# A block of products on constant tiles ahead of the first stage of a gated attention and feed-forward training step

## The chip, the core and the metric

One core of a Trainium2 chip runs the kernel. Five engines work side by side, each through its own list of instructions in order: TensorE (PE in the profile, its weight loads PEld), VectorE (DVE), ScalarE (ACT), GpSimd (POOL) and SyncE (SP). Transfers are issued from the queues of SP, ACT and POOL. Engines wait for each other through semaphores. The metric is the device time of one execution in microseconds, lower is better.

## What is computed

The reference is a mix of two branches on one input x (2048 rows, 512 columns, bf16), and the kernel returns the forward result and seven gradients:

```python
g = _sigmoid((x * gate_w).sum(-1, keepdims=True))
a = _A_ref(x, A_wqkv, A_wo)                  # attention, 32 heads of 16, window of 256, causal
b = _B_ref(x, B_W_gate, B_W_up, B_W_down)    # h = relu(x @ W_gate) * (x @ W_up), then h @ W_down, F = 1376
out = g * a + (1 - g) * b
...
_out, _vjp = jax.vjp(_f, A_x, A_wqkv, A_wo, B_W_gate, B_W_up, B_W_down, gate_w)
_grads = _vjp(grad_out)
```

The gradients are those of x, of the five weight matrices and of gate_w.

## The kernel before

The rows are cut into 16 tiles of 128, taken four at a time (tg, 512 rows: TGW), and the 1376 columns of the feed-forward branch into 11 pieces of 128 (fc). Three stages follow each other.

The first stage is the feed-forward branch forward and backward. 44 steps (11 pieces by 4 row groups) each make `gate` and `up` (products of Wg_sb and Wu_sb with x_T, L326), `dh` (product of WdT with db_T, L326 too), and six steps later the weight gradients (`weights`, L373 and L375). The results h and the two gradients are turned by transfers on SP's queue (`turn_h`, `turn_dgu`) and kept in memory by transfers on ACT's queue (`keep`). The second stage is attention: scores, exponentials, masks and their gradients, tile by tile, with the projections of later groups and the weight gradients laid between by a hand-written order with credits. The third stage takes two row tiles at a time and makes the output and the gradient of x.

Both the first and the second stage stand under an order written out by hand: instructions come on each engine in the order in which the code issues them.

Around the change the start of the first stage matters. In this order: VectorE fills the tile `warm` with zeros (L222); SP loads the first 512 rows of x in two halves (L225), while ACT's queue loads the first 256 columns of each weight (Wg_sb L226, Wu_sb L227) and gw_col (L228); ACT loads its table for the sigmoid (L230); POOL makes `ident`; PE does eight products of `warm` with itself, WARM = 8 (L234). Then SP loads the rest of x (L237) and the rows of grad_out (L213, into the tiles z), turns the first piece of W_down (L219) and loads the remaining columns of both weights (L247, L248). With the first rows there, `turn_x(0)` turns x on PE (tile ptx, L261), and VectorE and ACT each evict one half (L74, L72). Step 0 follows: `gate`, `turn_x(1)`, `up`, `gate_col` (L269, the tile zps, needs gw_col and gives g_all through a sigmoid), `db_rows` (L279 and L281, on ACT and VectorE), and a step later `turn_db` (tile ptd, L289). In the first four steps x and db are turned between the products; from then on a step is products alone.

The first-stage tiles db_r, db_T, Wg_sb, Wu_sb and gw_col come from the pool `acts` on the left side of the memory, which is opened with the stage; x_r, x_T and the z tiles lie elsewhere. The products' results lie in the pool ps1 of eight banks: three for products (tag mm), two for turns (tag tr), three for sums of weight gradients.

Of the kernel before, what the change touches and what calls it, by code (L numbers as in the profile page):

```python
# [11 lines left out]
BF = mybir.dt.bfloat16  # L12
F32 = mybir.dt.float32
I32 = mybir.dt.int32
PSUM = bass.MemoryType.PSUM
# [7 lines left out]
def kernel(  # L23
# [20 lines left out]
    nc = tc.nc  # L44
    P = 128
# [13 lines left out]
    TGW = min(512, S)  # L59
# [7 lines left out]
    def evac(out, in_, eng=None):  # L67
        if eng is None:
            eng = ("act", "dve")[rr["i"] % 2]
            rr["i"] += 1  # L70
        if eng == "act":
            nc.scalar.copy(out, in_)  # L72
        elif eng == "dve":
            nc.vector.tensor_copy(out, in_)  # L74
        else:
            nc.gpsimd.tensor_copy(out, in_)
# [36 lines left out]
    if True:  # L113
        HH = HG // 2
        proj = {}
        groups = [(c, tg) for c in range(DC) for tg in range(NTG)]
        PENG = ("dvs", "dvs")

        def project_parts(c, tg):
            t4 = {}  # L120
            proj[(c, tg)] = t4
            pj = pjA if (c * NTG + tg) % 3 == 0 else pjs["b"]

            def mm(nm, which, eng):
                ps, tag, bufs, _ = pools["now"]
                pp = ps.tile([P, TGW], F32, tag=tag, bufs=bufs, name="pp")
                for cd in range(DC):
                    if which < 3:
                        nc.tensor.matmul(pp[:], lhsT=w_p[c][:, cd, which * P:(which + 1) * P], rhs=x_T[tg][:, cd, :],  # L129
                                         start=(cd == 0), stop=(cd == DC - 1))  # L130
                    else:
                        nc.tensor.matmul(pp[:], lhsT=w_p[c][:, cd, 3 * P:4 * P], rhs=da_T[tg][:, cd, :],
                                         start=(cd == 0), stop=(cd == DC - 1))
                if nm in ("Q", "dO"):
                    if nm == "Q":
                        t4["z"] = pjA.tile([P, 2, TGW], BF, tag="zT", name="zT")
                    dst = t4["z"][:, ("Q", "dO").index(nm), :]
                else:
                    dst = pjA.tile([P, TGW], BF, tag="T", bufs=2, name=f"{nm}T")[:]
                if nm == "Q":  # L140
                    nc.vector.tensor_scalar(dst, pp[:], scale, None, op0=ALU.mult)
                else:
                    evac(dst, pp[:], eng)
                t4[nm] = dst
                if nm in ("Q", "dO"):
                    if c == 0 and tg == 0:
                        w = ("Q", "dO").index(nm)
                        for k in range(NP):
                            rows = slice(32 * k, 32 * k + 32)
                            evac(zt[0][rows, w, :, k, :], dst[rows, :].rearrange("p (k q) -> p k q", k=TPG),  # L150
                                 (("dve", "act")[w] if k % 2 else "dve"))
                else:
                    for k in range(2):
                        t4[f"{nm}{k}"] = pj.tile([P, TGW], BF, tag=f"{nm}{k}", name=f"{nm}{k}")
                        if PENG[k] == "act":
                            nc.scalar.mul(t4[f"{nm}{k}"][:], pp[:], par[:, k:k + 1])
                        elif PENG[k] == "dve":
                            nc.vector.tensor_scalar(t4[f"{nm}{k}"][:], pp[:], par[:, k:k + 1], None, op0=ALU.mult)
                        else:
                            nc.vector.tensor_scalar(t4[f"{nm}{k}"][:], dst[:], par[:, k:k + 1], None, op0=ALU.mult)  # L160

            def tr(a_nm, b_nm):
                ps, tag, bufs, trt = pools["now"]
                pt = ps.tile([P, 2, TPG, P], BF, tag=trt, bufs=2, name="ptp")
                for a, nm in enumerate((a_nm, b_nm)):
                    for k in range(TPG):
                        nc.tensor.transpose(pt[:, a, k, :], t4[nm][:, k * P:(k + 1) * P], ident[:])
                return pt

            def tr_rows():  # L170
                rows = pjA.tile([P, 2, TPG, P], BF, tag="rows", bufs=2, name="rows")
                nc.sync.dma_start_transpose(out=rows[:].rearrange("p a t d -> p (a t) d"),
                                            in_=t4["z"][:].rearrange("p a s -> p (a s)"))
                t4["rows"] = rows

            def tr_kv():
                kv = pj.tile([P, TPG, HG, 34], BF, tag="KV1", name="KV1")
                nc.gpsimd.memset(kv[:, :, :, 0:1], -1.0)
                nc.gpsimd.memset(kv[:, :, :, Dh + 1:Dh + 2], 1.0)
                pt = tr("K", "V")  # L180
                v = lambda a: pt[:, a, :, :].rearrange("p k (h d) -> p k h d", h=HG)
                nc.vector.tensor_scalar(kv[:, :, :, 1:1 + Dh], v(0), scale, None, op0=ALU.mult)
                nc.vector.tensor_copy(kv[:, :, :, Dh + 2:2 * Dh + 2], v(1))
                t4["kv"] = kv

            return [lambda: mm("Q", 0, "dve"), lambda: mm("dO", 3, "dve"), tr_rows, lambda: mm("K", 1, "act"),
                    lambda: mm("V", 2, "act"), tr_kv]

    with ExitStack() as p1, tc.manual_schedule():
        ps1 = p1.enter_context(tc.tile_pool(name="ps1", bufs=1, space=PSUM))  # L190
# [120 lines left out]
        for fc in range(FC):  # L311
            for tg in range(NTG):
                k = Step()
# [90 lines left out]
        for n in range(N1 + 8):  # L404
# [22 lines left out]
            if at(6):  # L427
                f = weights(at(6))
# [14 lines left out]
            if t in (NT + 3, NT + 5):  # L443
                i = (t - NT - 3) // 2
                nc.gpsimd.memset(zt[i][:, 0, :, :, :], 0.0)
                nc.vector.memset(zt[i][:, 1, :, :, :], 0.0)
            if n == N1 - 2:
                first = project_parts(*groups[0])
# [10 lines left out]
    if True:  # L459
# [340 lines left out]
        with tc.manual_schedule():  # L800
# [7 lines left out]
            n = 0  # L808
# [12 lines left out]
            while n <= NU + LAG or ev or cdq or bgq:  # L821
# [5 lines left out]
                if u is not None:  # L827
                    gi = u.c * NTG + u.j // TPG
                    if u.first and u.j == 0:
                        sts[u.c] = st.tile([P, NT, 4, P], BF, tag="rows_st", name="rows_st")  # L830
                    if u.first and u.j % TPG == 0:
                        if gi + 1 < len(groups):
                            prq = project_parts(*groups[gi + 1])
                            due = n + sum(2 * min(3, j + 1) for j in range(u.j, u.j + TPG)) - 3
                            if gi + 2 == len(groups):
                                due -= 10
                    if u.first and u.j == 6 and u.c > 0:
                        ev.setdefault(n + 1, []).append(("dma", lambda c=u.c - 1: spill(c, NT // 2)))
                    if u.first and u.j == 1 and u.c > 0:
                        ready = grad_parts(u.c - 1)  # L840
                    if u.first and u.j == TPG - 1 and u.c > 0:
                        bgq += ready
                    front(u)
                    if u.last and gi + 1 == len(groups) and u.j % TPG in (1, 3):
                        ev.setdefault(n + 2, []).append(("dma", lambda i=(u.j % TPG) // 2: early_f(i)))
# [7 lines left out]
                if LAG <= n < NU + LAG:  # L853
                    w = units[n - LAG]
# [65 lines left out]
    with ExitStack() as p56:  # L920
        x_r5 = x_r

        with ExitStack() as p6:
# [5 lines left out]
            for g in range(NG):  # L929
# [3 lines left out]
                for tl in range(GT):  # L933
# [4 lines left out]
                    for fc in range(FC):  # L938
                        nc.tensor.matmul(bps[:], lhsT=hT_g[:, fc, lsl], rhs=W6[("Wd", fc)],  # L939
                                         start=(fc == 0), stop=(fc == FC - 1))  # L940
                    aps = ps6.tile([P, D], F32, tag="aps", bufs=1)
                    for c in range(DC):
                        nc.tensor.matmul(aps[:], lhsT=T_g[:, 4 * c + 3, lsl], rhs=W6[("wo", c)],
                                         start=(c == 0), stop=(c == DC - 1))
# [20 lines left out]
                    i = 0  # L965
                    for src, wt in ((dgT_g, "Wg"), (duT_g, "Wu")):
                        for fc in range(FC):
                            nc.tensor.matmul(dxps[:], lhsT=src[:, fc, lsl], rhs=W6[(wt, fc)],  # L968
                                             start=(i == 0), stop=(i == nmm - 1))
# [14 lines left out]
                    for cc in range(C3):  # L984
                        nc.tensor.matmul(dxps[:], lhsT=T_g[:, 4 * (cc % DC) + cc // DC, lsl], rhs=W6[("wqkv", cc)],  # L985
                                         start=(i == 0), stop=(i == nmm - 1))
# [35 lines left out]
```

## Time and profile before

| | before |
|---|---|
| median of two runs | 978.9 us (978.26 to 979.54) |
| span of the profiled execution | 976.6 us |
| PE busy, products | 936.5 us, 11280 products |
| PE weight loads busy | 597.0 us |
| VectorE, ACT, POOL busy | 500.5, 473.1, 488.0 us |
| mean granted TensorE clock | 0.993 |
| moved by DMA | 161.6 MB, 166 GB/s on the mean |

A row of the profile's order of time has the start, the length, the engine, the line in the code, the operation, what it writes and reads by tile names, the array's part as rows*columns, the shape, the count of instructions taken together, and in brackets how long the engine was idle before it and what ended that. The length of a single product is counted to the end of its way through the array; products overlap, so the time between two starts, not the length, is what one product takes from the engine. PEld rows are the weight loads, which run beside products.

### The profile page before, as it was taken

The page shows a single profiled execution, that of the slowest core. Times are in us where ns is not written, and L with a number is a line of the kernel's source. Part 1 is how long each engine was busy: PE and PEld are TensorE (multiplying, and loading weights), DVE is VectorE, ACT ScalarE, POOL GpSimd, SP SyncE. Part 2 cuts the span into 40 slices and gives each one's busy share as a digit, 9 for nine tenths or more (in the row PEclk, how much of TensorE's full clock was granted, in tenths as well). Part 3 has the DMA queues.
Part 4 walks back from the last instruction along what each step waited for, and adds up shares of the span by engine and source line. Part 5 has one row for each costly group of instructions (what it writes and reads, how often), then busy time and mean ns, then how long its engine had stood idle before and what let it go on. Part 6 is the DMA issues. An engine that isn't in the chain of part 4 may idle for free.

```text
span 976.6 us, 27633 instructions
## 1 busy us (share of the span) xinstructions
PE 936.5 (96%) x11280; PEld 597.0 (61%) x11280; DVE 500.5 (51%) x918; ACT 473.1 (48%) x810; POOL 488.0 (50%) x935
## 2 busy tenths in 40 slices
PE   7999999999999999999999999989999999999993
PEld 4555555566567776677776777756777744444441
DVE  4443323233477776666776667756676513223221
ACT  5422322223377877667776767856667610001000
POOL 1644445444177667655676556665657612122220
PEclk9999999999999999999999999999999999999998
DMA  9989999987557688876789658799989898878810
GB/s 286 192 195 210 222 211 224 218 199 182 129 104 122 108 165 152 148 146 102 140 154 174 140 90 156 120 165 167 170 138 242 175 247 182 204 199 199 186 45 16
DMA packets 447935, 161.64 MB, mean 166 GB/s; under 512 B 366304, under 2 KB 445504, under 8 KB 447808
## 3 DMA queue, kind: packets, MB, share of 16 engines
q1 hardware_dynamic: 425408, 136.80, 72.0%
q10 hardware_dynamic: 20592, 17.84, 6.4%
q0 software_dynamic: 1808, 5.24, 1.5%
q8 instruction: 88, 1.44, 0.6%
q14 instruction: 39, 0.32, 0.1%
HBM read 38.44 MB, written 38.41 MB: 79 GB/s over the span
## 4 chain that ended last, share of the span: by engine, by line
PE 80%; DMA 5%; POOL 4%; DVE 2%; issue 2%; ACT 2%; SPq 2%; ACTq 0%; POOLq 0%; DVEq 0%
PE pt L706 9%; PE ST L649 7%; PE dxps L968 7%; PE dPT L669 7%; PE wps L373 6%; PE wps L588 4%; PE pp L129 4%; PE BA L683 4%; PE dxps L985 4%; PE bps L939 4%; PE CD L488 4%; PE dhps L326 3%; PE dps L375 3%; PE ups L326 3%; PE gps L326 3%
## 5 line engine op out<-in xcount | busy, mean ns | idle before, releaser
L674 DVE TENSOR_TENSOR Pd<-Pu,dPT 128x512 bf16<-128x512 bf16 x201 | 136.6, 681 | 63.7 <-POOL Pu L660 52.2
L655 ACT ACTIVATE Pu<-ST 128x512 bf16<-128x512 f32 x201 | 121.4, 606 | 57.4 <-PE ST L649 56.5
L649 PE MATMUL ST<-z,K 128*128 128x512 bf16 x360 | 136.2, 378 | 4.0 <-DVE Pd L674 1.5
L669 PE MATMUL dPT<-z,V 128*128 128x512 bf16 x360 | 136.3, 379 | 1.3 <-DVE Pd L674 1.1
L674 DVE TENSOR_TENSOR PP<-PP,dPT 128x512 bf16<-128x512 bf16 x159 | 108.4, 682 | 40.2 <-POOL PP L657 37.8
L655 ACT ACTIVATE PP<-ST 128x512 bf16<-128x512 f32 x159 | 95.7, 602 | 51.4 <-PE ST L649 41.3
L657 POOL TENSOR_SCALAR_AFFINE_SELECT PP<-PP 128x512 bf16<-128x512 bf16 x128 | 81.3, 635 | 78.4 <-ACT PP L655 77.6
L340 POOL TENSOR_TENSOR hT<-rg,upm 128x512 bf16<-128x512 bf16 x44 | 52.0, 1183 | 123.1 <-DVE upm L338 101.1
L488 PE MATMUL CD<-rq,p 128*128 128x32 bf16 x1440 | 109.4, 177 | 1.0 <-ACT rows_st L494 0.5
L373 PE MATMUL wps<-dgu_r,x_r 128*128 128x256 bf16 x704 | 105.6, 273 | 3.8 <-DVE wst L74 3.8
L491 PEld LDWEIGHTS <-p 128*128 128x128 bf16 x1440 | 86.1, 96 | 35.6 <-issue 2.4
L72 ACT COPY p<-pt 128x1024 bf16<-128x1024 bf16 x103 | 105.1, 1020 | 4.9 <-PE pt L706 2.4
L491 PE MATMUL CD<-rq,p 128*128 128x16 bf16 x1440 | 106.6, 169 | 0.0
L488 PEld LDWEIGHTS <-p 128*128 128x128 bf16 x1440 | 98.8, 96 | 1.7 <-issue 1.5
L660 POOL TENSOR_SCALAR_AFFINE_SELECT Pu<-Pu 128x512 bf16<-128x512 bf16 x112 | 71.0, 634 | 39.8 <-ACT Pu L655 39.2
L373 PEld LDWEIGHTS <-x_r 128*128 128x128 bf16 x704 | 68.8, 98 | 35.5 <-issue 4.9
L946 ACT COPY a_sb<-aps 128x512 f32<-128x512 f32 x16 | 9.4, 585 | 145.8 <-issue 133.1
L706 PE MATMUL pt<-ident,Pd 128*128 128x128 bf16 x804 | 78.1, 220 | 0.0
L706 PE MATMUL pt<-ident,Pu 128*128 128x128 bf16 x804 | 77.5, 218 | 0.0
L74 DVE COPY p<-pt 128x1024 bf16<-128x1024 bf16 x102 | 69.5, 681 | 5.4 <-PE pt L706 4.8
L332 ACT ACTIVATE rg<-gps 128x512 bf16<-128x512 f32 x44 | 26.3, 599 | 90.9 <-PE gps L326 39.3
L683 PE MATMUL BA<-KV,Pu 128*128 128x33 bf16 x804 | 66.5, 178 | 3.9 <-ACT BAs L689 3.8
(154 smaller groups left out, 1995.3 us busy)
## 6 DMA issues: line engine op xcount, KB each, us to landing
dqkvo_d<-rows_st SPq DMA_DIRECT2D x7, 1024.0 KB, 5.3
dar<-da_d SPq DMA_DIRECT2D x28, 256.0 KB, 4.4
hT_d<-hT ACTq DMA_DIRECT2D x44, 128.0 KB, 2.4
dgT_d<-dgu ACTq DMA_DIRECT2D x44, 128.0 KB, 2.8
duT_d<-dgu ACTq DMA_DIRECT2D x44, 128.0 KB, 2.9
duT_g<-duT_d SPq DMA_DIRECT2D x8, 640.0 KB, 5.3
dgT_g<-dgT_d SPq DMA_DIRECT2D x7, 640.0 KB, 5.2
gt<-hT_d SPq DMA_DIRECT2D x7, 640.0 KB, 5.7
```

The lines of the kernel that those rows point to most:

```text
L72: nc.scalar.copy(out, in_)
L326: nc.tensor.matmul(out[:], lhsT=w(c), rhs=x(c), start=(c == 0), stop=(c == DC - 1))
L373: nc.tensor.matmul(acc["w"][:, c, :], lhsT=x_r[:, t, c * P:(c + 1) * P], rhs=k.dgu_r[:, :, i, :], start=(go_ and c % 2 == 0), stop=no_, sk ...
L488: nc.tensor.matmul(cd[0][:, h, :], lhsT=p2[:, 0, hh, :], rhs=rq[:, h, 0:2 * Dh], start=cd[1], stop=True, skip_group_check=True)
L491: nc.tensor.matmul(cd[0][:, h, 0:Dh], lhsT=p2[:, 1, hh, :], rhs=rq[:, h, 2 * Dh:3 * Dh], start=False, stop=True, skip_group_check=True)
L649: nc.tensor.matmul(ST[:], lhsT=KTt[:, ksl], rhs=z[:, 0, jl, :, :], start=True, stop=True)
L655: nc.scalar.activation(u.Pu[:], ST[:], ACT.Exp)
L657: nc.gpsimd.affine_select(out=u.Pu[:], in_=u.Pu[:], compare_op=ALU.is_ge, fill=0.0, base=0, pattern=[[0, HH], [1, P]], channel_multiplier=-1)
L669: nc.tensor.matmul(u.dPT[:], lhsT=VTt[:, ksl], rhs=z[:, 1, jl, :, :], start=True, stop=True)
L674: nc.vector.tensor_tensor(out=u.Pd[:], in0=u.Pu[:], in1=u.dPT[:], op=ALU.mult)
L683: nc.tensor.matmul(BA[:, h, 0:33], lhsT=u.Pu[:, hh, :], rhs=kv[:, u.kb % TPG, h, 1:34], start=(u.first and hh == 0), stop=True, skip_group ...
L706: nc.tensor.transpose(pt[:, a, hh, :], src[:, hh, :], ident[:])
```

## The change

Ahead of the first stage, and after the definitions that the stages share, a block is put that opens two pools of its own: three tiles in the memory (td in bf16, 128 x 512, and tf and ti in 4-byte floats, 128 x 128) and eight result banks. VectorE fills td and tf with 0.5, and POOL makes ti an identity. PE then does 240 products: first 24 of full size and 512 columns, then twelve groups of small products, each followed by three full products of 256 columns (`mark`). The groups are

- 32-row products in the four row groups by turns, of 128, 512 and 384 columns (16, 8, 16 of them), and four rounds of four 32-row products of 128 columns and one full product of 512
- 64-row products in two row groups by turns, of 128 and 512 columns (8 and 8)
- 16 full products of 128 columns, and 16 products of 128 columns all in row group 0
- 8 transposes of a 4-byte tile
- 16 products of 32 output rows in the four column groups by turns, 128 columns
- 32-row products in turns again, of 256 columns (16) and 64 columns (32)

No result is read. Both pools are closed before the first stage's are opened, so that the first stage's tiles and banks take the same places. What the kernel computes stays the same.

```diff
--- before.py
+++ after.py
@@ -185,6 +185,67 @@
 
             return [lambda: mm("Q", 0, "dve"), lambda: mm("dO", 3, "dve"), tr_rows, lambda: mm("K", 1, "act"),
                     lambda: mm("V", 2, "act"), tr_kv]
+
+    with ExitStack() as p0, tc.manual_schedule():
+        tp = p0.enter_context(tc.tile_pool(name="tp", bufs=1))
+        tps = p0.enter_context(tc.tile_pool(name="tps", bufs=1, space=PSUM))
+        NB = 8
+        tb = [tps.tile([P, TGW], F32, name=f"tb{i}") for i in range(NB)]
+        td = tp.tile([P, TGW], BF, name="td")
+        tf = tp.tile([P, P], F32, name="tf")
+        ti = tp.tile([P, P], F32, name="ti")
+        nc.vector.memset(td[:], 0.5)
+        nc.vector.memset(tf[:], 0.5)
+        make_identity(nc, ti[:])
+
+        def mm(bank, r0, k, n, m0=0, m=P, c0=0):
+            rows = slice(r0, r0 + k)
+            nc.tensor.matmul(tb[bank][m0:m0 + m, c0:c0 + n], lhsT=td[rows, 0:m], rhs=td[rows, 0:n], start=True, stop=True,
+                             skip_group_check=True)
+
+        def mark(n=3, w=256):
+            for _ in range(n):
+                mm(7, 0, P, w)
+
+        mark(24, 512)
+        for i in range(16):
+            mm(i % 4, 32 * (i % 4), 32, P)
+        mark()
+        for i in range(8):
+            mm(i % 4, 32 * (i % 4), 32, TGW)
+        mark()
+        for i in range(16):
+            mm(i % 4, 32 * (i % 4), 32, 384)
+        mark()
+        for g in range(4):
+            for i in range(4):
+                mm(i, 32 * i, 32, P)
+            mm(7, 0, P, TGW)
+        mark()
+        for i in range(8):
+            mm(i % 2, 64 * (i % 2), 64, P)
+        mark()
+        for i in range(8):
+            mm(i % 2, 64 * (i % 2), 64, TGW)
+        mark()
+        for i in range(16):
+            mm(i % 4, 0, P, P)
+        mark()
+        for i in range(16):
+            mm(0, 0, 32, P, c0=P * (i % 4))
+        mark()
+        for i in range(8):
+            nc.tensor.transpose(tb[i % 4][:, 0:P], tf[:], ti[:])
+        mark()
+        for i in range(16):
+            mm(i % 4, 0, P, P, m0=32 * (i % 4), m=32)
+        mark()
+        for i in range(16):
+            mm(i % 4, 32 * (i % 4), 32, 256)
+        mark()
+        for i in range(32):
+            mm(i % 4, 32 * (i % 4), 32, 64)
+        mark()
 
     with ExitStack() as p1, tc.manual_schedule():
         ps1 = p1.enter_context(tc.tile_pool(name="ps1", bufs=1, space=PSUM))
```

Lines behind the block are 61 higher in the changed kernel: the warm-up of L234 is at L295, the loads of L226 to L228 at L287 to L289. The block's products are recorded at L203, its transposes at L238.

## The prediction

> **What bounds the kernel now.** I read first the page's busy times and slices, then the order of time over the first 35 us, where the edit stands, then busy time by stretches, groups by shape, and the DMA issues of the start.
>
> ```profile
> span 976.6 us, 27633 instructions
> ...
> PE   7999999999999999999999999989999999999993
> ```
>
> TensorE (PE) works for 936.5 of 976.6 us (96%). Only the first and the last slice hold idle time worth the name, so whatever is put on PE ahead of the first stage lengthens the span unless it fills the idle time of slice one. The order of time on PE: start, length in us, engine, line, tile, count, and in brackets the idle time before it and who ended it.
>
> ```profile
> 1.27 3.51 PE L234 MATMUL warm_ps<-warm 128*128 128x512 bf16 x8 [1.27 <-DVE tiny L229]
> 4.62 0.61 PE L261 MATMUL ptx<-ident,x_r 128*128 128x128 bf16 x8
> 5.76 0.62 PE L261 MATMUL ptx<-ident,x_r 128*128 128x128 bf16 x8 [0.53 <-DMA x_r<-in_A_x_dram]
> 7.48 1.02 PE L326 MATMUL gps<-x,Wg_sb 128*128 128x512 bf16 x4 [1.10 <-ACT x L72]
> 9.88 1.07 PE L261 MATMUL ptx<-ident,x_r 128*128 128x128 bf16 x16 [1.38 <-DMA x_r<-in_A_x_dram]
> 10.79 1.03 PE L326 MATMUL ups<-x,Wu_sb 128*128 128x512 bf16 x4
> 11.65 0.54 PE L269 MATMUL zps<-gw_col,x 128*128 128x1 bf16 x16
> 12.05 1.02 PE L326 MATMUL gps<-x,Wg_sb 128*128 128x512 bf16 x4
> 13.59 1.07 PE L261 MATMUL ptx<-ident,x_r 128*128 128x128 bf16 x16 [0.51 <-DMA x_r<-in_A_x_dram]
> ...
> 18.61 1.05 PE L261 MATMUL ptx<-ident,x_r 128*128 128x128 bf16 x16 [0.94 <-DVE db_T L74]
> ```
>
> The first product of the first stage starts at 7.48 us. After it PE waits twice for rows of x (1.38 and 0.51) and once for VectorE (0.94). The weight loads of the warm-up, in the same order, give the pace of the start:
>
> ```profile
> 1.67 0.15 PEld L234 LDWEIGHTS <-warm 128*128 128x128 bf16 x1 [0.28 <-issue]
> ...
> 3.81 0.15 PEld L234 LDWEIGHTS <-warm 128*128 128x128 bf16 x1 [0.28 <-issue]
> ```
>
> By stretches (PE's busy time comes after the length):
>
> ```profile
> 22.00:35.00 13.00, 13.00 (x100) 7.07 (x98) 9.25 (x15) 8.73 (x15) 8.50 (x8) 1.00 1.15 230
> ```
>
> From 22 us on PE is full, so a delay at 22 us reaches the end whole. Last, the length of one product by shape (mean ns behind the busy time), and the loads of the start (last number: us from issue to landing):
>
> ```profile
> L326 PE MATMUL gps<-x,Wg_sb 128*128 128x512 bf16 x176 | 45.2, 379 | 1.4 <-ACT x L72 1.1 <-ACT rg L332 0.3
> L261 PE MATMUL ptx<-ident,x_r 128*128 128x128 bf16 x64 | 4.4, 219 | 3.4 <-DMA x_r<-in_A_x_dram 2.4 <-DVE db_T L74 0.9
> ```
> ```profile
> Wg_sb<-in_B_W_gate_dram ACTq DMA_DIRECT2D x1, 256.0 KB, 4.1
> Wu_sb<-in_B_W_up_dram ACTq DMA_DIRECT2D x1, 256.0 KB, 5.4
> ...
> gw_col<-in_gate_w_dram ACTq DMA_DIRECT2D x1, 1.0 KB, 8.4
> ```
>
> **Prices.** Products are pipelined, so the price is the pitch, the time between starts. Four of 512 columns take 1.02 to 1.03 us of which the last is 0.379: pitch 0.217. Sixteen of 128 take 1.07: (1.07 - 0.219) / 15 = 0.057. Four of 256 (L373, at 35.07 us) take 0.60, the last 0.273: 0.109. Sixteen of one column take 0.54, the last 0.163: 0.025, the least seen. For 384 columns I put three quarters of 512: 0.163. Each product lasts 0.162 us beyond its pitch (0.379 - 0.217, 0.219 - 0.057): that is what emptying the array costs once. At the start the pitch is doubled: from the load at 1.67 to that at 3.81 there are five steps of 0.428.
>
> **The block on PE.** It is 240 products, and in the changed program they stand ahead of everything else on PE. Its start waits for VectorE's fill of td, 512 two-byte elements, which begins at 0.94; the fill of warm began there and took 0.27 as 256 four-byte ones, so 0.27 to 0.54: PE begins at about 1.5. First 24 full products of 512 columns: eight at 0.428 and sixteen at 0.217, 6.9. Thirty-six marks of 256: 3.9. Two runs of 16 products of 128 columns that can't overlap (the full ones, and the ones on row group 0 alone): 1.8. Together 12.6.
>
> The products on part of the array (32 or 64 rows, or 32 columns) have no row in this trace: every shape in it reads 128*128. If they take turns as full ones do, by pitch: 16 of 128 columns 0.9; 8 of 512 1.7; 16 of 384 2.6; four rounds of four of 128 and one full 512 1.8; 64-row ones 0.5 and 1.7; column groups 0.9; 16 of 256 1.7; 32 of 64 columns (0.029, a little over the least pitch) 0.9: 12.8 unrounded. If neighbours in different groups run side by side, four at a time (two for 64 rows) and never under a pitch of 0.025: 0.4, 0.5, 0.65, 1.3, 0.2, 0.9, 0.4, 0.4, 0.8: 5.6. Neighbours use other rows, other partitions of td and another bank, and so share nothing; I take 5.6 and keep 12.8 for the range. The Trainium skill (TensorE: Matmul & The Clock Gate, Part 3) gives a speedup of 3.07 for four row groups at 512 columns; by it the 8 of 512 would take 1.7 / 3.07 = 0.57, an estimate, and no run here shows it yet.
>
> Eight 4-byte transposes bring their own weights in the same instruction. Low end: the pitch of a 2-byte one, 8 x 0.057 = 0.5. High end: a weight load (0.097 in the groups' rows) and a whole product of 0.219 one after the other, doubled for the bytes: 0.63 each, 5.1. I take 0.25 each, nearer to one load and one unhidden product: 2.0.
>
> Between a partial group and a full product the array's division changes 26 times (in and out of nine groups, and of each of the four rounds). Low end nothing, high end emptying at each, 26 x 0.162 = 4.2; unable to tell, I take 2.1. The array's end adds 0.2. The Trainium skill (TensorEngine Tiling (Array Packing), Key Properties) says that changing the tiling mode drains TensorE; by it the 4.2 would stand whole and the sum would be 2.1 higher, which no run here shows yet.
>
> The block ends at T = 1.5 + 12.6 + 5.6 + 2.0 + 2.1 + 0.2 = 24.0 us.
>
> **What it moves.** The block's tiles td, tf and ti lie where the first stage's weights lie afterwards. In the changed program's list the first slice of Wg_sb (ACT queue) and the rest of it (SP queue) wait for semaphores that the list of before lacks: VectorE's, Pool's and PE's at 240, the whole block. Queued behind this on ACT: the slices of Wu_sb, gw_col, the table load (1.28), the second half of x's eviction; on SP: the rest of Wu_sb, then the h_r transposes, which need hT anyway. The loads of x and of grad_out stay free and land under the block, so the waits of 1.38 and 0.51 go. Pool's and VectorE's few fills (under 0.6 each) lie under it too. Apart from the 240 products and four fills no engine's order differs.
>
> After T: the warm-up, now at full pitch, 8 x 0.217 = 1.7; 16 transposes, 1.0; ACT is free after 0.5 + 0.55 + 0.53 of issues, 1.28 of table and 0.2, at T + 3.2, and evicts x until T + 4.2. Wg_sb's slice lands at T + 4.2 as before, or later: 1120 KB of the rest of Wg_sb now start beside it. Wu_sb's follows, then gw_col at T + 1.1 + 8.4 = T + 9.5, where zps waits for it (before it landed at 10.3, and was needed at 11.4). The work up to it (gate 0.9, transposes 1.1, up 0.9 after T + 4.2) would be through at T + 7.0. So zps stands at T + 7.0 to T + 9.5; before, its loads began at 11.4. The shift there is T - 4.4 to T - 1.9; 0.5 of waiting for x is then saved, while VectorE's 0.94 stays. T - 4.9 to T - 2.4, and I take T - 3.0, as the late load is the likelier: 24.0 - 3.0 = 21.0 us.
>
> The profiled run's span is 976.6 with 2.3 us around it, which is the median of 978.9; 978.9 + 21.0 = 999.9, say 1000.
>
> **Rivals.** A change of 2%, about what a measurement of this kernel can tell from no change, is 19.6 us: 998.5 is the line.
>
> Side by side and free: no emptying at the 26 changes, and transposes at 0.057. T = 1.5 + 12.6 + 5.6 + 0.5 + 0.2 = 20.4, shift 17.4, 996.3, not slower by that line (994.4 if gw_col is early). It decides from T under 22.6. For it: full products of mixed shapes (128x512 beside 128x33) follow each other in this trace at their own pitch; against: none changes the division.
>
> In turn: partial products cost a full pitch. T = 24.0 + 7.2 = 31.2, shift 28.2, 1007. For it: it is the only thing the trace shows of products; against: they share no rows and no bank.
>
> In turn and emptied at every change of group: 136 products x 0.162 = 22.0 in place of the 2.1: T = 51, 1027. Nothing in the trace has such gaps: even transposes with a new weight each time keep 0.057.
>
> No block at all (unused results left out): 979. The changed program holds all 240 products, so nearly excluded.
>
> **How the numbers follow.** Forecast 0.50, by the spread of its unknowns (drains 0 to 4.2, transposes 0.5 to 5.1, gw_col) 997 to 1004; free 0.23, 994 to 998.5; in turn 0.20, 1003 to 1010; emptied 0.05; no block and the like 0.02. The likeliest gives 1000. Slower by over 2%: 0.20 + 0.05 + four fifths of 0.50 = 0.65; faster 0.01; within 2% the other 0.34. From 994.5 to 1010 some 0.12 is left out.
>
> **What would show it.** The first warm_ps at T = 24.0, with a pitch of 0.217; groups of four 32-row products starting within 0.1 us of each other where side by side, 0.217 apart at 512 columns where in turn; a gap up to 0.16 between a partial group and the mark; Wg_sb's slice issued only when the block is over; zps waiting for gw_col some 9 us after T; from 22 us after T - 3 on, the same rows as before, shifted whole. A T outside 20 to 32, or a shift that shrinks or grows after the first stage, makes this wrong.

## The result, and the profile after

The changed kernel takes 1007.5 us (median of 1006.5 and 1008.5) against 978.9: 28.6 us slower by the medians where 21.1 had been forecast, and inside the range of 994.5 to 1010. The ratio that the comparison gives is 1.0272 with an interval of 1.0237 to 1.0307, which is 26.6 us of 978.9. Two further comparisons on other occasions gave 1.0266 (1.0239 to 1.0292) and 1.0253 (1.0228 to 1.0278), 25 to 26 us. The profiled execution has a span of 1006.7 us, 30.1 above that of before.

The page's head and its slices of PE:

```profile
span 1006.7 us, 28122 instructions
...
PE   9799999999989999999999999989998999999993
```

The first slice is now full, and the second, where the first stage begins, is the one with idle time. The order of time on PE (start, length, line, tile; in brackets the idle time before it and who ended it):

```profile
1.54 17.26 PE L203 MATMUL tb<-td 128*128 128x512 bf16 x156 [1.54 <-DVE td L197]
18.64 1.04 PE L238 MATMUL tb<-ti,tf 128*128 128x128 f32 x8
19.51 3.02 PE L203 MATMUL tb<-td 128*128 128x256 bf16 x76
22.59 1.89 PE L295 MATMUL warm_ps<-warm 128*128 128x512 bf16 x8
24.31 1.06 PE L322 MATMUL ptx<-ident,x_r 128*128 128x128 bf16 x16
29.76 1.89 PE L387 MATMUL gps<-x,Wg_sb 128*128 128x512 bf16 x4 [4.39 <-DMA Wg_sb<-in_B_W_gate_dram]
31.44 1.64 PE L322 MATMUL ptx<-ident,x_r 128*128 128x128 bf16 x16
32.95 1.04 PE L387 MATMUL ups<-x,Wu_sb 128*128 128x512 bf16 x4
33.82 0.54 PE L330 MATMUL zps<-gw_col,x 128*128 128x1 bf16 x16
...
40.13 1.05 PE L322 MATMUL ptx<-ident,x_r 128*128 128x128 bf16 x16 [0.54 <-DVE db_T L74]
```

The block's last product starts at 22.26 us, and the first product of the warm-up, whose start is the prediction's T, at 22.59. (The expectations below count the block's end, 22.3, by the first weight load of the warm-up, also at 22.26.) The warm-up and the turns of x follow as forecast; then PE stands still for 4.39 us until the slice of Wg_sb is there. The loads of the start (KB each, us from issue to landing):

```profile
Wg_sb<-in_B_W_gate_dram SPq DMA_DIRECT2D x1, 1120.0 KB, 6.3
...
Wg_sb<-in_B_W_gate_dram ACTq DMA_DIRECT2D x1, 256.0 KB, 7.1
Wu_sb<-in_B_W_up_dram ACTq DMA_DIRECT2D x1, 256.0 KB, 9.8
...
gw_col<-in_gate_w_dram ACTq DMA_DIRECT2D x1, 1.0 KB, 9.6
```

The slice needs 7.1 us instead of 4.1: in the trace, packets of 512 bytes (the slices, on ACT's queue) and of 2240 bytes (the rest, on SP's queue) pass in equal numbers, some 135 of each per us, from 25 to 31 us. And the four gate products after the wait run at half the clock. In the stretch below the granted clock is the last column but two; the trace has it halved from 29.2 to 32.6 us:

```profile
29.70:31.50 1.80, 1.74 (x5) 0.64 (x6) 0.00 (x0) 0.00 (x0) 0.00 (x0) 0.50 1.09 367
```

Inside the block the weight loads show the partial groups, since each group's loads carry its rows (32*128: 32 rows of the array):

```profile
9.45 0.12 PEld L203 LDWEIGHTS <-td 32*128 32x128 bf16 x8 [0.21 <-issue]
9.99 0.22 PEld L203 LDWEIGHTS <-td 128*128 128x128 bf16 x3 [0.42 <-issue]
10.43 0.45 PEld L203 LDWEIGHTS <-td 32*128 32x128 bf16 x16 [0.21 <-issue]
11.19 0.22 PEld L203 LDWEIGHTS <-td 128*128 128x128 bf16 x3 [0.32 <-issue]
11.62 0.26 PEld L203 LDWEIGHTS <-td 32*128 32x128 bf16 x5 [0.21 <-issue]
12.11 0.26 PEld L203 LDWEIGHTS <-td 32*128 32x128 bf16 x5 [0.23 <-issue]
12.60 0.26 PEld L203 LDWEIGHTS <-td 32*128 32x128 bf16 x5 [0.23 <-issue]
```

Eight 32-row products of 512 columns stand between 9.45 and 9.99, 0.54 us; at a full pitch they would need 1.74. Sixteen of 384 take 0.76 (10.43 to 11.19) against 2.61. A round of four partial products and one full takes 0.49 (11.62 to 12.11). By the starts of single products in the trace, four neighbours begin 0.003 to 0.005 us apart and the next four one pitch after the first; a full product after a partial one, or the other way round, begins 0.10 us later than its pitch (for example 0.205 instead of 0.109 after a full product of 256 columns).

### The late growth

The instructions on VectorE are the same 918 in both kernels but for two fills, so each can be set beside its counterpart. Its start in the trace minus that in the first profile of before, at five places named by their time in before:

| kernel, profile | 41 us | 300 us | 740 us | 770 us | 961 us | growth |
|---|---|---|---|---|---|---|
| before, second | 0.0 | 0.9 | 0.0 | 2.0 | 2.0 | 2.0 |
| before, third | -0.6 | 0.4 | 0.4 | 0.9 | 0.9 | 1.5 |
| before, fourth | 1.4 | 2.7 | 3.5 | 6.4 | 6.4 | 5.0 |
| changed, first | 21.0 | 23.4 | 24.9 | 28.0 | 28.0 | 7.0 |
| changed, second | 22.8 | 24.9 | 25.5 | 28.0 | 28.0 | 5.2 |
| changed, third | 21.9 | 22.8 | 24.1 | 27.2 | 27.2 | 5.3 |

So 21 to 23 us are paid in the first 41 us, and 5 to 7 arise later, in steps at 100 to 245, 640 to 660 and 752 us. Two lines of the waits (us in total, times, longest), of before and after:

```profile
PE BA L683 <- ACT BAs L689: 7.4, 9, 2.6
PE wps L373 <- DVE wst L74: 3.8, 4, 1.3
```
```profile
PE BA L744 <- ACT BAs L750: 9.0, 10, 3.3
PE wps L434 <- DVE wst L74: 5.3, 4, 1.7
```

These two waits are the largest of before too, and in these two profiles each is longer by some 1.5 us after the change. They arise where the DMA engines are full: their share in before is 0.92 from 100 to 200 us, 1.02 from 640 and 1.20 from 745 on. Over all profiles the sum of the two waits is 11.2, 12.0, 12.6 and 13.2 us before and 14.3, 13.6 and 13.9 us after the change: 1.7 us more in the mean.

The granted clock has a part in it too. Two stretches at about the same place of the work, the first of before, the second of the changed kernel (granted clock again the last column but two):

```profile
755.00:765.00 10.00, 9.97 (x208) 8.00 (x207) 7.95 (x14) 8.20 (x14) 7.94 (x19) 1.00 1.08 194
780.00:790.00 10.00, 9.97 (x175) 7.42 (x173) 6.28 (x11) 7.88 (x13) 7.44 (x18) 0.83 1.07 186
```

Between the table's first and last place the traces have the clock halved for 3.4, 6.8, 3.4 and 6.8 us in the four profiles of before and for 6.8, 10.2 and 10.2 us in the three of the changed kernel. In these seven every such period comes during or within 1.4 us after a wait of PE for BAs of 2.2 us or more, and every such wait has one. It costs up to half its length, which is up to 2.0 us more in the mean after the change. The step at 752 us is of this kind: with a halved clock there it is 2.0 to 3.1 us in five profiles, without it 0.5 in the third of before.

### The profile page after: what moved, and what is told of

Its sections match the earlier page's. It is cut to its first block, busy times and chain, and to the rows that moved or that the text cites. A ratio compares the mean times of both kernels' runs of the same rounds, so it can differ in the third digit from the quotient of the medians.

```text
span 1006.7 us, 28122 instructions
## 1 busy us (share of the span) xinstructions
PE 958.9 (95%) x11520; PEld 608.9 (60%) x11520; DVE 500.1 (50%) x920; ACT 473.0 (47%) x810; POOL 488.8 (49%) x937
## 4 chain that ended last, share of the span: by engine, by line
PE 78%; DMA 5%; POOL 3%; DVE 3%; issue 2%; ACT 2%; SPq 2%; ACTq 0%; POOLq 0%; DVEq 0%
PE pt L767 8%; PE ST L710 7%; PE dxps L1029 7%; PE dPT L730 7%; PE wps L434 6%; PE wps L649 4%; PE pp L129 4%; PE BA L744 4%; PE dxps L1046 4%; PE CD L549 4%; PE bps L1000 4%; PE ups L387 3%; PE dps L436 3%; PE dhps L387 3%; PE gps L387 3%
```

## The experiments

**Repeats.** Three more profiles of the kernel before and two of the changed one, unedited.

> The kernel before once more, to see how far two executions of one kernel differ. Both theories of the late growth (from 21.1 us of shift at 100 us to 28.0 at 765 us): if it is an accident of single executions, this profile's waits of PE for the eviction of wst (3.8 us in four waits before) and for BAs (7.4 us in nine) move by 1 to 3 us against the first profile and the time stays 978 to 980; if the growth is owed to the block, they stay within 0.5 us.

> The changed kernel once more. Accident: the steps of the shift at 120, 165, 245, 640 to 690 and 752 us don't return at the same places, and the time lies 21 to 27 us above before. Owed to the block: the same steps return, 27 to 29 us above before. In both the block's own end stays at 22.3 us, for its pitches do not hang on data or neighbours.

> The kernel before, a third execution with a profile, for the late growth: against the first profile the shift of the kernels with a block grew by 2.5 to 7.0 us after 41 us, that of the second profile of before by 2.0. Accident: growth between 0 and 5. Owed to the block: within 0 to 2 again.

> The kernel before, a fourth execution with a profile. Accident: growth of the shift after 41 us, against the first profile, anywhere between 0 and 5 us. Owed to the block: within 0 to 2 us as in the second profile.

> The changed kernel a third time. Accident: growth after 41 us against the first profile of before anywhere from 1 to 7 us. Owed to the block: 5 to 7 again.

The kernel before gave 980.5, 980.8 and 981.8 us (ratios to itself 1.0011, 1.0004, 0.9999), the changed one 1006.2 and 1006.1. The table above holds the profiles. The first profile of before was the one without growth: its own repeats grow by 1.5 to 5.0 at the same places. So part of the 7.0 is accident of single executions. The signs that had been named do not separate the theories: in the second profile of before the wait for wst moved by 0.9 us and that for BAs by 0.1, between the two expectations; the changed kernel's second comparison lay 25.7 us above before, in the range named for accident; the 5.0 of the fourth speaks for accident, and the 5.3 of the changed kernel's third fits both. But all three profiles of the changed kernel lie above all of before, if by 0.2 us at the nearest, and the timings agree: 25 to 27 us, where the first 41 us account for 21.7 (the mean of 21.0, 22.8 and 21.9, less the mean 0.2 of the four profiles of before). Some 3 to 5 us of growth therefore go with the change. The expectation that the block ends at 22.3 us each time failed: in the second profile thirteen products ran at half pace ahead of the turn to full pace instead of nine, and it ended some 0.9 us later; in the third it ended 0.7 us later.

**The weights free to load.**

```diff
-        tp = p0.enter_context(tc.tile_pool(name="tp", bufs=1))
...
-        td = tp.tile([P, TGW], BF, name="td")
-        tf = tp.tile([P, P], F32, name="tf")
-        ti = tp.tile([P, P], F32, name="ti")
+        td = cpool.tile([P, TGW], BF, name="td")
+        tf = cpool.tile([P, P], F32, name="tf")
+        ti = cpool.tile([P, P], F32, name="ti")
```

> td, tf and ti in the pool of constants, so that no later tile takes their place and the first weights load at once. Theory late load: the block still ends at 22.3 us, the first gate product starts at about 26.4 instead of 29.8 (eviction of x is then last), at full pitch, and the time falls by 3.4 for the wait and some 1.0 for the products at half pace: 4 to 5 us under the changed kernel. Rival (the load is hidden, the time is the block's alone): within 1 us of the changed kernel. If the late growth too came from the order of the loads, it falls by up to 12 us.

It took 1000.3 us, ratio 1.0202 (1.0176 to 1.0229), 5.9 under the changed kernel of the same comparison. Order of time on PE:

```profile
25.06 1.06 PE L321 MATMUL ptx<-ident,x_r 128*128 128x128 bf16 x16
27.22 1.02 PE L386 MATMUL gps<-x,Wg_sb 128*128 128x512 bf16 x4 [1.10 <-ACT x L72]
```

The gate products start 2.2 us after the turns of x instead of 5.5 and take 1.02 instead of 1.89. The block itself ended later than expected (the warm-up starts at 23.34), with more products at half pace at its head. The shift at 41 us is 17.1; it still grows by 6.8 to the end. So the wait for the weights is real and costs 5 to 6 us. The late growth is there without it, as far as one profile can tell.

**The slices alone.**

```diff
-        nc.sync.dma_start(Wg_sb[:, :, W0:F], Wg_v[:, :, W0:F])
-        nc.sync.dma_start(Wu_sb[:, :, W0:F], Wu_v[:, :, W0:F])
...
             if at(1):
                 turn_h(at(1))
+            if n == 1:
+                nc.sync.dma_start(Wg_sb[:, :, W0:F], Wg_v[:, :, W0:F])
+                nc.sync.dma_start(Wu_sb[:, :, W0:F], Wu_v[:, :, W0:F])
```

> The changed kernel with the loads of the rest of Wg_sb and Wu_sb moved behind the first h_r transposes on SP's queue, so that the first slices load alone. Theory late load: the slice of Wg_sb lands within 4 us of the block's end instead of 7.1 us after its issue, the first gate product starts some 4 us after the block (x's eviction is last), without products at half pace; 4 to 5 us faster than the changed kernel, 1000 to 1002. Rival (the slice is late for its own 512-byte rows, not for the company): under 1 us of difference.

1000.5 us, ratio 1.0191 (1.0172 to 1.0210). The slice and the gate:

```profile
Wg_sb<-in_B_W_gate_dram ACTq DMA_DIRECT2D x1, 256.0 KB, 3.0
```
```profile
26.26 1.02 PE L385 MATMUL gps<-x,Wg_sb 128*128 128x512 bf16 x4 [1.29 <-ACT x L72]
```

The block ends as before (the warm-up starts at 22.19), the weights still wait for it, and yet the slice lands 3.0 us after its issue, with up to 619 packets of 512 bytes per us, and the eviction of x is last. The shift at 41 us is 16.1 against 21.0. So it was the company of the rest that made the slice late; the wait behind the block alone costs next to nothing, as the turn of x takes as long.

**Only full products.**

```diff
         mark(24, 512)
-        for i in range(16):
-            mm(i % 4, 32 * (i % 4), 32, P)
-        mark()
...
+        mark(63, 512)
```

> In place of the twelve groups and their marks 63 full products of 512 columns, 13.6 us at 0.217, so that the block ends at 22.3 us as before with none but full products; the loads still wait for it. Theory time alone: the same time as the changed kernel within 1 us, and the same start of the first stage. Rival (partial products leave something behind, in the array or in the clock): 2 us or more below it.

1005.1 us, ratio 1.0281 (1.0247 to 1.0316), against 1.0266 (1.0239 to 1.0292) for the changed kernel of the same comparison: the same within the intervals. Growth 4.6 us. Within the 3 us that these intervals leave, what the block holds does not matter beyond its length.

**Everything waits.**

```diff
-        td = tp.tile([P, TGW], BF, name="td")
+        td = x_r[:, 0, :]
...
-        nc.vector.memset(td[:], 0.5)
+        nc.vector.memset(td, 0.5)
```

> td lies in the first row tile of x, so that the loads of x and of grad_out wait for the block as well and the whole start of the kernel is moved behind it. Theory order of the transfers (the late growth of 4 to 7 us comes from the transfers standing otherwise against PE): the start repeats that of before, gate begins some 7 us after the block's end, the shift is 21 to 22 us in the first stage and grows by no more than 2 us, as between two executions of before; 1000 to 1003. Rival (any delay brings the growth): 4 us or more of growth, 1005 to 1008.

1005.0 us, ratio 1.0235 (1.0213 to 1.0257); shift at 41 us 21.3, growth 4.0. The first theory's growth of at most 2 us and its 1000 to 1003 did not come; 4.0 and 1005.0 lie just at the rival's lower bounds. But a repeat of the unchanged kernel grew by 5.0, so one profile does not decide it.

**The price of a change of the array's division.** 40 rounds of four 32-row products and a full one were added to the four of the block; in the second kernel the same products were sorted.

```diff
-        for g in range(4):
+        for g in range(44):
```

> The round of four 32-row products and one full product of 512 columns is done 44 times instead of 4, 80 changes of the array's division more. Theory (each change empties the array, 0.10 us, and the total pays it): 40 x 0.489 = 19.6 us above the changed kernel. Rival (the gap in the records is how their ends are modelled and PE does not lose it): 40 x (0.055 + 0.216) = 10.9 us above.

1027.0 us, ratio 1.0463 (1.0439 to 1.0487), 0.0191 to 0.0210 above the changed kernel's three ratios, 19 to 21 us. The warm-up starts 19.7 us later than the changed kernel's 22.59:

```profile
42.29 1.89 PE L295 MATMUL warm_ps<-warm 128*128 128x512 bf16 x8
```

It is the theory's 19.6, not the rival's 10.9: PE does lose the 0.10 us at each change.

```diff
             for i in range(4):
                 mm(i, 32 * i, 32, P)
+            mm(7, 0, P, TGW)
+        for g in range(40):
+            for i in range(4):
+                mm(i, 32 * i, 32, P)
+        for g in range(40):
             mm(7, 0, P, TGW)
```

> The same products as with 44 rounds, but of the 40 added rounds all 160 partial products first and then the 40 full ones, so that two changes are added instead of 80. Both theories: 40 x 0.055 + 40 x 0.216 + 0.2 = 11.1 us above the changed kernel; against the 44 rounds it is 8.5 us faster by the theory, the same by the rival.

1023.9 us (1019.3 to 1026.2), 3.1 under the 44 rounds: this expectation failed, for both theories. The reason stands on PE:

```profile
14.30 0.94 PE L203 MATMUL tb<-td 32*128 32x128 bf16 x54
18.11 2.31 PE L203 MATMUL tb<-td 32*128 32x128 bf16 x33 [2.86 <-issue]
```

In the middle of the dense run PE stands for 2.86 us without waiting for any engine or transfer, after which the granted clock is halved for 3.4 us. A packet of 16384 bytes on the queue of instructions falls into the standstill, at 15.45 us. The changed kernel has such a packet at 15.70 without a standstill, but there PE had begun 235 products and weight loads by then, here 449. The reading that fits is that the sorted products outran the loading of their own instructions; it was not tried by itself and is not shown. The standstill and the half pace after it (2.86 and about half of 3.4) take 4.6 of the 8.5 us that the theory had, and the warm-up indeed starts at 38.03, 4.3 before that of the 44 rounds.

**All on one group.**

```diff
-            mm(i % 4, 32 * (i % 4), 32, P)
+            mm(i % 4, 0, 32, P)
...
-            mm(i % 2, 64 * (i % 2), 64, P)
+            mm(i % 2, 0, 64, P)
...
-            mm(i % 4, 0, P, P, m0=32 * (i % 4), m=32)
+            mm(i % 4, 0, P, P, m0=0, m=32)
```

> The same 240 products, but all partial ones on the first row group (or the first column group), the banks as they were. Theory (the groups' products run side by side because they lie in different groups): they now follow each other at the pitch of full ones, 0.056, 0.217, 0.163, 0.109 and 0.029 us by columns; the nine groups take 14.4 us instead of 6.0, the block ends at 30.6 and the time rises by 8.3. Rival (they run side by side because they write different banks or hold fewer rows): no difference.

1025.2 us, ratio 1.0443 (1.0411 to 1.0475): 17 to 19 us above the changed kernel, twice the 8.3 that the theory had. The weight loads:

```profile
10.48 1.40 PEld L203 LDWEIGHTS <-td 32*128 32x128 bf16 x8 [0.21 <-issue]
12.31 0.22 PEld L203 LDWEIGHTS <-td 128*128 128x128 bf16 x3 [0.42 <-issue]
```

and the stretches (length, PE busy, PEld, DVE, ACT, POOL, granted clock, DMA share, GB/s):

```profile
9.06:12.70 3.64, 3.64 (x31) 1.97 (x30) 0.00 (x0) 0.00 (x0) 0.00 (x0) 1.00 1.10 348
13.00:17.00 4.00, 4.00 (x14) 1.80 (x13) 0.00 (x0) 0.00 (x0) 0.00 (x0) 0.50 1.05 334
17.00:36.00 19.00, 19.00 (x97) 10.79 (x96) 0.00 (x0) 0.00 (x0) 0.00 (x0) 0.50 0.00 1
37.00:41.50 4.50, 4.50 (x70) 3.49 (x67) 0.00 (x0) 0.00 (x0) 0.00 (x0) 1.00 0.02 4
```

The theory holds where the clock is full: the 512-column group takes 1.83 us (10.48 to 12.31) instead of 0.54, with the same banks and rows per product. So the groups, not the banks, let products run side by side. From 12.9 to 36.8 us the clock was halved, although PE is busy throughout in the profile. Half of these 23.9 us, 11.9, with the 8.3 makes about the 19.5 us by which the block ends later (41.76 instead of 22.26). It is no accident of one execution: the mean granted clock of all four is 0.973 to 0.980, that of the changed kernel's 0.986 to 0.993. The Trainium skill (TensorE: Matmul & The Clock Gate, Part 1) ties the half rate to a window in which PE is idle; here it came with PE busy, after partial products had run one after the other on one row group since 9.05 us. Which of the products bring it about was not separated; the full products and the transposes in those 23.9 us did not end it.

## Why the prediction was right

The direction is right and the time inside the stated range. But 1007.5 us lies outside the 997 to 1004 of the forecast's own mechanism, and just where the rival "in turn" had been priced (1007). By the time alone the wrong one would have been chosen; what decides are the starts on PE.

**The block, 24.0 forecast, 22.6 measured.** PE begins at 1.54 (1.5). The 24 full products take 7.05 (6.9), nine at half pace. The marks keep 0.109. "I take 5.6" for products side by side was the right choice of the two ends and still too long: by the starts in the trace they need about 4.4, since the least pitch of 0.025 was the wrong floor; neighbours in other groups begin 0.003 to 0.005 apart. The 4-byte transposes cost 0.109 each, 0.87 in all, not 2.0: near the low end. Each change of division costs 0.10, which agrees with neither end: 26 make 2.6, not 2.1 and not 4.2. The trace agrees with the Trainium skill (TensorEngine Tiling (Array Packing), Key Properties) that changing the tiling mode drains TensorE. The price here is 0.10 us, less than the 0.162 that a product lasts beyond its pitch, which the prediction had as its high end.

**What it moves, T - 3.0 forecast, T - 1.5 measured (21.05 at 41 us).** The warm-up at full pitch, the turn of x and ACT's eviction until T + 4.0 (26.6; forecast T + 4.2) stand as worked out. The step that failed is "Wg_sb's slice lands at T + 4.2 as before, or later": it landed at T + 7.1, gw_col at T + 10.7 instead of T + 9.5, and zps stood at T + 11.2, outside T + 7.0 to T + 9.5. zps did not wait for gw_col, which had been forecast: what held it up was the wait for the slice. VectorE's 0.94, which was to stay, became 0.54. The company in loading had been named and priced at nothing for the slice; that the wait of 4.4 us would go with a clock halved from 29.2 to 32.6 us was missed.

The two errors, 1.4 too much for the block and 1.5 too little behind it, cancel: 21.0 was forecast for the first stage and 21.05 stands there. The right sum at that place is in part luck.

**"The same rows as before, shifted whole"** failed, and by the prediction's own sign (a shift that grows after the first stage) that part is wrong: the shift grows by 5 to 7 us against the profile that was used. That profile was the fastest of four in its late part; its repeats grow by 1.5 to 5.0 themselves. In the mean the growth is 5.8 us after the change and 2.1 before. Of the 3.7 between them the longer waits for wst and BAs hold 1.7, and the longer time at a halved clock up to 2.0. Why the waits are longer, whether from any delayed start or from the order of the transfers, stays open: the kernel in which everything waits grew by 4.0, the one with free weights by 6.8, the one with the slices alone by 3.7, and single executions differ by as much.

**Rivals.** "Side by side and free" had the products and nearly the transposes right, and fell by the 2.6 us of emptying together with the late slice; "in turn" is, where its clock was full, what the kernel on one group did, not this one. All three comparisons of the changed kernel have intervals above 1.02.

## What to carry to other kernels

A tile that is used early and freed can hold back the loads that take its place, and what then starts together on two queues passed packet for packet here, the small load as slowly as the large one: put small urgent loads ahead of large ones in time, not only on another queue. Products on part of the array paid here only with neighbours in different groups, and mixing them with full ones cost 0.10 us at every change. Before a shift of some microseconds is explained, look at the same steps in repeats of the unchanged kernel, and at the granted clock at the same place.

## What had not been expected of the hardware

- PE's clock fell to half with PE busy throughout, in the kernel whose partial products ran one after the other on one group (granted 0.50 from 12.9 to 36.8 us); in the block with groups side by side it stayed at 1.00.
- PE stood for 2.86 us in a dense run of partial products with nothing to wait for that the profile shows; that their instructions were not loaded yet is a reading, not shown.
- The 4-byte transposes with their own weights keep a pitch of 0.109 us, twice the 0.057 of the 2-byte ones.
- A longer wait of PE can cost more than its length: each wait of 2.2 us or more for BAs, in the seven profiles of the two kernels, goes with 3.4 or 6.8 us at half the clock. This is no fixed bound: in four of the other kernels' profiles waits of 1.45 to 2.1 us go with one, and in a fifth a wait of 2.25 us does not.
